# The second layer's input matrix is converted last, through small buffers of its own

## Chip, cores and metric

The kernel runs on one core of one Trainium2 chip. The metric is the device time of one execution in microseconds (us). Engines: PE is TensorE, DVE is VectorE, ACT is ScalarE, POOL is GpSimd, SP is SyncE, which issues the DMAs here.

## What is computed

Attention that keeps the 32 largest scores of each row, then two feed-forward layers with different activations:

```python
scores = q @ k.T / sqrt(64)                       # 4 batches, 8 heads, 576 rows
kth = np.partition(scores, -32, axis=-1)[..., -32:-31]
scores = np.where(scores >= kth, scores, -1e9)
x = softmax(scores) @ v                           # -> 2304 tokens x 512
h = x @ w_in1;  x = np.maximum(0.01 * h, h) @ w_out1        # 512 -> 2048 -> 512
h = x @ w_in2;  r = np.maximum(h, 0)
out = (s * r * r + b) @ w_out2                    # 512 -> 2048 -> 512
```

All is float32. The kernel gets near it from float16 products: each operand is split into a high and a low half (hi, lo), and a product is three matmuls, hi·hi + hi·lo + lo·hi.

## The kernel before

**Attention.** The 2304 tokens are 18 tiles of 128 rows; tiles 4 and 13 each take the last 64 rows of two batches (half-array matmuls). A tile has 4 units of two heads, so there are 72 units, numbered 0 to 71. Of each unit PE makes the scores (`qk`, L1056), ACT copies them out (`s_ev`, L1062), and DVE finds the 32 largest per row: for each head four `MAX8` (L1074) and three `MATCH_REPLACE8` (L1083). ACT and POOL, or for some units DVE (`mask`, L1099), make the masked exponentials; `e_hi` (ACT) and `e_lo` (POOL) split them, a transposing DMA turns them, `pv_mm` (PE, L1224) multiplies with v, and `x_ev` (DVE, L1231) writes the tile's quarter of x.

**The weights.** The four matrices, named 1i, 1o, 2i, 2o (layer, in or out), are converted at the start beside the first tiles of attention, each as 16 units of 128x1024 words (64-bit inputs in, 128x512 float32 kept). A unit is loaded into ring `raw` (`w_load`, L543), brought to float32 (`w_rest` and `w_sign` on ACT, `w_shift` on DVE, `w_round` on POOL), and after four units a Gram matrix on PE (`w_norm`, L594) and some tiny DVE steps give the scale of the group. With it the unit is split into hi and lo. Table `WM` names the way for each unit: A (scale and hi on ACT, lo on POOL), D (hi on ACT, `lo_d` on DVE, L701), G (scale on DVE, hi on ACT, lo on POOL), P and V (a float32 matmul `lo_t` on PE, L706, hi on ACT, lo on PE and ACT for P, on DVE for V). Layer 1's halves stay in SBUF in `wreg`. Layer 2's go to DRAM (`w_out`, L749, tensors `sc16`) out of a ring `hl` of 8, and are streamed back for each block.

`ORDER` (L29) says in which order the matrices pass: 2o, 2i, 1i, 1o. The rings overlay each other: `hl` and the float32 units (`wT`) of 2o, 2i and 1i lie in `wreg` itself, so layer 1's halves can be written only as layer 2's are gone; 1o has a ring `T` of 10.

**The layers.** `layer(i, l, ...)` (L1309) works on one tile for layer 1 (l = 0) and on a block of two tiles for layer 2 (l = 1). PE makes h from x and w_in (`m_in`, L1349), ACT applies the activation from PSUM (`a1`, L1378 and L1381), for layer 2 the square is made twice (`a3`, in float32, on ACT at L1388 or POOL at L1390 as table `SQ` says, and `a4`, its high half), POOL makes the low half (`a5`, L1397), and PE multiplies with w_out (`m_out`, L1419). `finals1` (L791 to L795, DVE) makes layer 1's activation scales, once 1i and 1o have theirs; `finals` (L809 to L823) makes layer 2's, once all matrices are converted and written. `a1` of layer 1 can't start before `finals1`, nor that of layer 2 before `finals`. At `finals` the conversion's buffers close and those of the stream open (`open_phase`). Ring `xT1` holds layer 2's input for two blocks, so layer 1 can be at most four tiles ahead of layer 2.

**The order.** Every step is given to `Plan.add` with its engine and the steps it depends on; `Plan.order` (L311) then emits all of them by a table of ranks, `AT` (L90 to L255), held back only by dependencies and free buffers. So the order of each engine's and of SP's instructions is fixed by numbers, and each engine works its queue strictly in that order.

Of the kernel before, what the change touches and what calls it, by code (L numbers as in the profile page):

```python
# [1530 lines left out]
```

## Time and profile before

| | |
|---|---|
| median of 3 runs | 1139.66 us (1135.37 to 1141.71) |
| the profiled execution | 1141.21 us |
| its span on the core | 1139.1 us |
| mean granted TensorE clock | 0.953 of full speed |
| PE busy | 1041.4 us, 91% of the span |
| DVE busy | 913.2 us, 80% |
| ACT busy | 874.4 us, 77% |
| POOL busy | 797.6 us, 70% |

The span is what the trace shows; the profiled execution's time has 2.1 us around it. An engine's share is an average over stages: conversion with attention, then attention with layers, then layers alone. Waits tell more than shares.

### The profile page before, as it was taken

To read this page: it belongs to the slowest core of one execution; us is meant where nothing else is said; L and a number is where in the kernel's file an instruction comes from. 1 tells how busy PE (TensorE), PEld (TensorE's weight loads), DVE (VectorE), ACT (ScalarE), POOL (GpSimd) and SP (SyncE) were. 2 spreads that over 40 slices of the span, in tenths; PEclk is the share of its full clock that TensorE was granted. 3 is DMA by queue.
4 is the path that set the end of the run, shared out by engine and by line. 5 is a ranking of instruction groups with operands and counts; after the bars stand their busy time and mean duration, and the time that the engine had idled before them with its cause. 6 is when DMAs were issued, how large, how long until landed. Compare 5 with 4: busy or idle time off the path is not lost.

```text
span 1139.1 us, 27433 instructions
## 1 busy us (share of the span) xinstructions
PE 1041.4 (91%) x10254; PEld 727.4 (64%) x10254; DVE 913.2 (80%) x2209; ACT 874.4 (77%) x1653; POOL 797.6 (70%) x1126
## 2 busy tenths in 40 slices
PE   3667676789989999999999999999999999999998
PEld 2334333476756677777767777777777777677665
DVE  3999999999977999999989999982999999710000
ACT  7898999988776977888997986887679677733332
...
PEclk9878688599989999999999999999999999999999
...
GB/s 274 292 179 212 248 310 247 118 81 96 175 152 265 166 102 165 219 150 115 146 224 208 137 238 149 97 101 220 151 158 227 145 81 75 190 160 29 156 188 146
DMA packets 352549, 193.43 MB, mean 170 GB/s; under 512 B 284576, under 2 KB 309152, under 8 KB 352416
## 3 DMA queue, kind: packets, MB, share of 16 engines
...
## 4 chain that ended last, share of the span: by engine, by line
PE 60%; DVE 15%; ACT 11%; DMA 6%; POOL 5%; issue 3%; SPq 1%; DVEq 0%; ACTq 0%; POOLq 0%
PE h L1349 26%; PE acc L1419 24%; DVE mx L1074 5%; DVE wk L1083 4%; PE sc L1056 4%; PE pv L1224 4%; DMA a<-ehl 2%; ACT em L1115 1%; POOL em L1112 1%; DMA st_i<-sc_2i 1%; POOL ehl L1190 1%; DVE wreg L556 1%; DVE em L1099 1%; ACT ehh L1184 1%; DMA late<-in_moe_w_out_dram 1%
## 5 line engine op out<-in xcount | busy, mean ns | idle before, releaser
L1074 DVE MAX8 mx<-wk 128x8 f32<-128x576 f32 x432 | 314.9, 750 | 1.6
L1419 PEld LDWEIGHTS <-late 128*128 128x128 f16 x1728 | 160.4, 98 | 135.0 <-issue 3.0
L1349 PEld LDWEIGHTS <-wreg 128*128 128x128 f16 x3456 | 210.1, 98 | 40.2 <-issue 3.9
L1349 PE MATMUL h<-early,wreg 128*128 128x128 f16 x3456 | 227.5, 220 | 3.0 <-ACT late L1378 2.2
L1419 PE MATMUL acc<-wreg,late 128*128 128x512 f16 x864 | 218.8, 379 | 0.0
L1083 DVE MATCH_REPLACE8 wk<-mx,wk 128x576 f32<-128x576 f32 x288 | 212.9, 743 | 0.0
L1190 POOL TENSOR_TENSOR ehl<-em,ehh 128x576 f16<-128x576 f32 x136 | 175.7, 1296 | 32.0 <-ACT ehh L1184 17.6
L1419 PE MATMUL acc<-st_o,late 128*128 128x512 f16 x756 | 191.6, 380 | 0.5 <-DMA st_o<-sc_2o 0.5
L1349 PE MATMUL h<-late,st_i 128*128 128x256 f16 x1512 | 182.9, 274 | 1.7 <-DMA st_i<-sc_2i 1.7
L1349 PEld LDWEIGHTS <-st_i 128*128 128x128 f16 x1512 | 147.7, 99 | 37.6 <-DMA st_i<-sc_2i 4.7
L1112 POOL TENSOR_TENSOR em<-s,em 128x576 f32<-128x576 f32 x98 | 139.2, 1433 | 26.0 <-ACT em L1109 25.5
L1397 POOL TENSOR_TENSOR late<-early,late 128x512 f16<-128x512 f32 x72 | 84.1, 1168 | 88.4 <-ACT early L1388 54.1
L1397 POOL TENSOR_TENSOR late<-late 128x512 f16<-128x512 f32 x72 | 85.2, 1185 | 47.2 <-ACT late L1394 47.2
L1074 DVE MAX8 mx<-s 128x8 f32<-128x576 f32 x144 | 107.3, 750 | 10.5 <-ACT s L1062 9.8
L1062 ACT COPY s<-sc 128x576 f32<-128x576 f32 x144 | 91.2, 633 | 29.9 <-PE sc L1056 29.7
L1056 PE MATMUL sc<-kT,qT 128*128 128x288 f16 (+1 forms) x640 | 98.4, 294 | 9.5 <-ACT s L1062 6.8
L1083 DVE MATCH_REPLACE8 wk<-mx,s 128x576 f32<-128x576 f32 x144 | 106.8, 743 | 0.0
L1394 ACT ACTIVATE late<-late 128x512 f16<-128x512 f32 x144 | 90.0, 626 | 9.8 <-PE acc L1419 8.1
L1381 ACT ACTIVATE late<-h,cg 128x512 f32<-128x512 f32 x72 | 49.2, 684 | 62.4 <-PE h L1349 61.9
L1184 ACT CAST ehh<-em 128x576 f16<-128x576 f32 x136 | 90.3, 668 | 5.6 <-DVE em L1099 4.9
L1109 ACT ACTIVATE em<-s,st 128x576 f32<-128x576 f32 x98 | 74.1, 771 | 25.6 <-POOL st L1103 25.2
L1115 ACT ACTIVATE em<-em,st,est 128x576 f32<-128x576 f32 x98 | 84.7, 864 | 9.6 <-POOL em L1112 9.0
(217 smaller groups left out, 1657.5 us busy)
## 6 DMA issues: line engine op xcount, KB each, us to landing
...
qn<-in_q_dram SPq DMA_DIRECT2D x16, 256.0 KB, 3.9
sc_2o<-wreg SPq DMA_DIRECT2D x16, 256.0 KB, 4.7
sc_2i<-wreg SPq DMA_DIRECT2D x16, 256.0 KB, 5.5
out_dram<-o SPq DMA_DIRECT2D x16, 256.0 KB, 2.5
```

Source lines behind the costliest of these rows:

```text
L1056: nc.tensor.matmul(pt[a, c, 0:288], lhsT=qT[u][:, h, z, a], rhs=kT[b, p][:, 576 * h + 288 * c:576 * h + 288 * c + 288], start=(z == 0), st ...
L1062: nc.scalar.copy(sc[u, h], box["pt"][:, :, 0:288])
L1074: nc.vector.max(out=mx[u][:, h, r, :], in_=wk[u, h] if r else flat(sc[u, h]))
L1083: nc.vector.match_replace(out=wk[u, h], in_to_replace=mx[u][:, h, r, :], in_values=src, imm_value=NEG)
L1112: nc.gpsimd.tensor_tensor(em[u][:, h, :], flat(sc[u, h]), em[u][:, h, :], op=ALU.subtract)
L1115: nc.scalar.activation(em[u][:, h, :], em[u][:, h, :], AF.Exp, bias=st[u][:, h:h + 1], scale=est[:, 0, u:u + 1], accum_out=st[u][:, 2 + h: ...
L1184: nc.scalar.copy(ehl[u][0][:, 576 * h:576 * h + 576], em[u][:, h, :])
L1190: nc.gpsimd.tensor_tensor(ehl[u][1][:, a], em[u][:, h, :], ehl[u][0][:, a], op=ALU.subtract)
L1349: nc.tensor.matmul(box["h"][:, n * T:(n + 1) * T], lhsT=w[:, ew, c, :], rhs=src[:, ex, c, :], start=(c == 0 and ew == 0 and ex == 0), stop ...
L1394: nc.scalar.activation(gt[:, 0], box["r1"], AF.Square if l else AF.Copy)
L1397: nc.gpsimd.tensor_tensor(ghl[i, l, g][:, 1], box["v"], ghl[i, l, g][:, 0], op=ALU.subtract)
L1419: nc.tensor.matmul(accs[i, l, tt], lhsT=ghl[i, l, g][:, eg, n * T + tt * P:n * T + (tt + 1) * P], rhs=w[:, ew], start=(f == 0 and eg == 0 ...
```

## The change

ORDER becomes 2o, 1i, 1o, 2i. So `finals1` needs only what is converted before 2i, and layer 1 of the first tiles can run while 2i is still converted. For that 2i no longer uses `wreg`: its raw units have a ring `raw2` of 2 (the shared `raw` goes from 5 to 4), its float32 units take ring `T` (from 10 to 8, after 1o), and its halves go out of a ring `hl2` of 1 for ways A, D and G, or in place for V and P. Besides: one group of 2o (units 4 to 7) is brought to float32 by three DVE steps (`w_bits`, `w_top`, `w_tail`) in place of the ACT, DVE and POOL steps; the ways of the units change (`WM`); three of four squares of layer 2 move from ACT to POOL (`SQ`); tables `MK`, `MKE`, `KVM`, `IDM` and `WR` shift a few steps between engines; and `AT` is new throughout. The durations in the `add` calls play no part once `AT` is given.

```diff
-... "xT1": 2, "r1": 2, "r2": 2, "g": 3, "raw": 5, "T": 10, "hl": 8, "wT": 24, "wst": 4,
+... "xT1": 2, "r1": 2, "r2": 2, "g": 3, "raw": 4, "raw2": 2, "T": 8, "hl": 8, "hl2": 1, "wT": 24, "wst": 4,
...
-WM = {"1i": "PPPPPVVPPVPVGVVV", "1o": "ADAAADGAAAAAADAG", "2o": "VPVVPPVVAPVVVPVV", "2i": "PPPPPPPGGPPPPAPA"}
-ORDER = ("2o", "2i", "1i", "1o")
-WJ = {"1i": "SSSS", "1o": "SSSS", "2o": "SSSS", "2i": "SSSS"}
+WM = {"1i": "PPPPGGVPPVPGGDDD", "1o": "AAAAAGPAAAAAAPPP", "2o": "PVVVVPPVAPVGVVPP", "2i": "AAADADADDVVDVVDD"}
+ORDER = ("2o", "1i", "1o", "2i")
+WJ = {"1i": "SSSS", "1o": "SSSS", "2o": "SBSS", "2i": "SSSS"}
...
-SQ = "AAAA"
-MK = "AADADA"
-MKE = "AADAADDADAAAAAAADADAAAAD"
-KVM = "DGDGGDGDDGGGGGGG"
+SQ = "GGAG"
+MK = "DAAADA"
+MKE = "DAAAADDADAAAAAAADADAADAD"
+KVM = "DGDGGGDDDGGGGGGG"
...
 AT = [
-    0, 7, 9, 12, 13, 2, 14, 15, 16, 17, 3, 18, 20, 21, 23, 4, 24, 31, 25, 32, 38, 39, 50, 51, 52, 75, 79, 81, 93, 94, 117, 80, 85, 98, 101, 111,
...
-    PHASED = ("wst", "raw", "T", "nred")
+    PHASED = ("wst", "raw2", "T", "nred")
...
-              "wT": (flat_w, 8 * 512), "hl": (flat_w, 0), "cI": (early, 2560),
+              "wT": (flat_w, 8 * 512), "hl": (flat_w, 0), "hl2": (early, 2048), "cI": (early, 2560),
...
-        w = wreg[:, f + (NU if m[1] == "o" else 0), :] if m[0] == "1" else hl[m, f]
+        w = wreg[:, f + (NU if m[1] == "o" else 0), :] if m[0] == "1" else hl.get((m, f), wT[m, f])
...
-            t = ring("raw", [P, 1024], I32, f"raw_{m}_{f}")
+            t = ring("raw2" if m == "2i" else "raw", [P, 1024], I32, f"raw_{m}_{f}")
...
-            wT[m, f] = ring("T" if m == "1o" else "wT", [P, 512], F32, f"T_{m}_{f}")
+            wT[m, f] = ring("T" if m in ("1o", "2i") else "wT", [P, 512], F32, f"T_{m}_{f}")
...
+        if m == "1i" and f >= 8:
+            modes = [x if x in "PV" else "V" for x in modes]
...
-            out_tok = [token("hl")] if m[0] == "2" else []
+            out_tok = [token("hl")] if m == "2o" else [token("hl2")] if m == "2i" and mode in "GAD" else []
...
-                free = [lo_done["1i", ff]]
-            elif m == "1i":
-                free = [lo_done["2i", ff]] if ff >= 8 else [out_done[order[24 + ff]], cs_done.get(order[24 + ff])]
+                free = [lo_done["2o", 8 + ff] if ff < 8 else lo_done["1i", ff - 8]]
+            elif m == "1i" and ff < 8:
+                free = [out_done["2o", 8 + ff], cs_done.get(("2o", 8 + ff))]
```

What moves, at three places. The first is DVE just ahead of `finals1`, whose first row is the `TENSOR_REDUCE` of `consts`. Before:

```order
L497 TENSOR_SCALAR cg_89<-gram_1o_3_2370 128x1
L718 TENSOR_TENSOR wreg_64<-wlo_1i_15_2399,wreg_64 128x512
L502 TENSOR_SCALAR cg_89<-cg_89 128x1
L1074 MAX mx_11_2404<-s_11_1_2416 128x8
L1083 MATCH_REPLACE wk_11_0_2409<-mx_11_2404,wk_11_0_2409 128x576
L1083 MATCH_REPLACE wk_11_1_2483<-mx_11_2404,s_11_1_2416 128x576
L1074 MAX mx_11_2404<-wk_11_0_2409 128x8
L1074 MAX mx_11_2404<-wk_11_1_2483 128x8
L1083 MATCH_REPLACE wk_11_0_2409<-mx_11_2404,wk_11_0_2409 128x576
L1083 MATCH_REPLACE wk_11_1_2483<-mx_11_2404,wk_11_1_2483 128x576
L786 TENSOR_REDUCE consts_88<-cg_89 128x1
```

and now:

```order
L494 TENSOR_SCALAR cg_89<-gram_1o_3_1830 128x1
L1076 MAX mx_8_1800<-wk_8_0_1807 128x8
L499 TENSOR_SCALAR cg_89<-cg_89 128x1
L719 TENSOR_TENSOR wreg_64<-wlo_1i_13_1856,wreg_64 128x512
L553 SCALAR_TENSOR_TENSOR T_2i_0_1869<-raw_2i_0_197,rest_2i_0_1870 128x512
L719 TENSOR_TENSOR wreg_64<-wlo_1i_12_1816,wreg_64 128x512
L1085 MATCH_REPLACE wk_8_1_1859<-mx_8_1800,wk_8_1_1859 128x576
L1233 TENSOR_TENSOR x32_1_1617<-pv_6_1880,st_6_1458 128x128
L553 SCALAR_TENSOR_TENSOR T_2i_1_1876<-raw_2i_1_218,rest_2i_1_1877 128x512
L1076 MAX mx_8_1800<-wk_8_1_1859 128x8
L1076 MAX mx_9_1974<-s_9_0_1952 128x8
L788 TENSOR_REDUCE consts_88<-cg_89 128x1
```

`finals1` has moved from the middle of unit 11's search to that of units 8 and 9, and only two units of 2i have reached float32 ahead of it. The second place is DVE just ahead of `finals`. Before:

```order
L1074 MAX mx_16_3502<-wk_16_0_3537 128x8
L1083 MATCH_REPLACE wk_16_1_3562<-mx_16_3502,wk_16_1_3562 128x576
L1231 TENSOR_TENSOR x32_3_3296<-pv_14_3642,st_14_3093 128x128
L1074 MAX mx_16_3502<-wk_16_1_3562 128x8
L1139 RECIPROCAL st_15_3322<-st_15_3322 128x2
L1074 MAX mx_17_3726<-s_17_0_3670 128x8
L1099 SCALAR_TENSOR_TENSOR em_16_3703,st_16_3503<-s_16_0_3405,mx_16_3502,em_16_3703 128x576
```

and now:

```order
L1076 MAX mx_19_4408<-wk_19_1_4464 128x8
L719 TENSOR_TENSOR T_2i_12_3706<-wlo_2i_12_4469,T_2i_12_3706 128x512
L1085 MATCH_REPLACE wk_19_1_4464<-mx_19_4408,wk_19_1_4464 128x576
L702 SCALAR_TENSOR_TENSOR early_63<-T_2i_15_4156,cg_89,early_63 128x512
L1085 MATCH_REPLACE wk_19_0_4425<-mx_19_4408,wk_19_0_4425 128x576
L1076 MAX mx_19_4408<-wk_19_1_4464 128x8
L1076 MAX mx_19_4408<-wk_19_0_4425 128x8
L1085 MATCH_REPLACE wk_19_1_4464<-mx_19_4408,wk_19_1_4464 128x576
```

`finals` has moved back from the end of unit 16 to that of unit 19, right behind the last halves of 2i. The third place is ACT in the middle of 2i's halves (`early` is where `hl2` lies). Before, where P units take two ACT copies out of PSUM into a ring of 8:

```order
L712 CAST wreg_64<-wlo_2i_9_1537 128x512
L712 CAST wreg_64<-wlo_2i_10_1554 128x512
L552 ACTIVATE rest_1i_11_1616<-late_65 128x512
L1096 ACTIVATE em_6_1609<-s_6_1_1436,st_6_1401,est_94 128x576
L715 CAST wreg_64<-wlo_2i_9_1537 128x512
```

and now:

```order
L688 ACTIVATE early_63<-T_2i_3_2234,cg_89 128x512
L1186 CAST ehh_13_3193<-em_13_3106 128x576
L1117 ACTIVATE em_13_3106,st_13_2788<-em_13_3106,st_13_2788,est_94 128x576
L1064 COPY s_15_0_3204<-sc_15_0_3145 128x576
L1186 CAST ehh_13_3193<-em_13_3106 128x576
L1064 COPY s_15_1_3221<-sc_15_1_3210 128x576
L686 CAST early_63<-T_2i_4_2598 128x512
```

The high half of unit 4 stands six ACT rows behind that of unit 3 and writes the same buffer.

## Rows read from the trace of the kernel before

**Rows 1.** The page, parts 1 and 2: engines, and PE and its clock in 40 slices
```profile
PE 1041.4 (91%) x10254; PEld 727.4 (64%) x10254; DVE 913.2 (80%) x2209; ACT 874.4 (77%) x1653; POOL 797.6 (70%) x1126
...
PE   3667676789989999999999999999999999999998
...
PEclk9878688599989999999999999999999999999999
```

**Rows 2.** Windows: stretch, length, then PE, PEld, DVE, ACT, POOL busy us; PEclk; DMA share
```profile
0.00:57.00 57.00, 29.95 (x125) 16.66 (x126) 36.95 (x98) 46.52 (x93) 31.53 (x46) 0.91 0.96 283
57.00:232.40 175.40, 124.97 (x812) 70.37 (x811) 171.97 (x415) 165.96 (x322) 138.78 (x185) 0.76 0.80 217
232.40:307.00 74.60, 70.12 (x870) 52.22 (x867) 71.72 (x166) 62.10 (x119) 67.36 (x89) 0.98 0.51 99
307.00:370.00 63.00, 56.91 (x545) 40.05 (x546) 49.37 (x122) 45.52 (x92) 38.98 (x68) 0.95 0.87 220
370.00:769.00 399.00, 393.39 (x4354) 288.69 (x4353) 381.73 (x931) 335.56 (x638) 322.91 (x480) 1.00 0.75 158
769.00:1139.10 370.10, 366.07 (x3558) 259.39 (x3556) 201.51 (x481) 218.77 (x394) 198.06 (x262) 1.00 0.59 148
```

**Rows 3.** Timeline of DVE: last row of finals1, first and last of finals
```profile
236.28 1.14 DVE L795 SCALAR_TENSOR_TENSOR cg<-cg 128x4 f32<-128x4 f32 x1
...
299.78 0.15 DVE L786 TENSOR_REDUCE consts<-cg 128x1 f32<-128x4 f32 x1
...
306.08 0.16 DVE L822 TENSOR_TENSOR consts<-consts,sb 128x1 f32<-128x1 f32 x1
```

**Rows 4.** Timeline of PE: layer 2's first matmuls
```profile
307.00 1.47 PE L1349 MATMUL h<-late,kept_i 128*128 128x256 f16 x12 [0.47 <-issue]
```

**Rows 5.** The chain in order of time: start, us, engine and line, count; pieces at full pace
```profile
81.56 1.72 PE wlo_2o L706 x2
...
308.68 1.32 DVE mx L1074 x2
310.00 1.46 DVE wk L1083 x2
...
412.70 1.34 PE h L1349 x24
414.04 1.94 PE acc L1419 x9
...
763.02 1.87 PE pv L1224 x52
```

**Rows 6.** Groups by line: busy us, mean ns of one, idle before
```profile
L1397 POOL TENSOR_TENSOR late<-early,late 128x512 f16<-128x512 f32 x72 | 84.1, 1168 | 88.4 <-ACT early L1388 54.1 <-ACT late L1394 27.2 <-issue 5.9
L1388 ACT ACTIVATE early<-late 128x512 f32<-128x512 f32 x72 | 44.7, 621 | 1.2
L565 ACT ACTIVATE late<-late 128x512 f32<-128x512 f32 x52 | 35.1, 684 | 0.8
L556 DVE SCALAR_TENSOR_TENSOR wreg<-late,rest_2i 128x512 int32<-128x512 int32 x13 | 8.5, 671 | 0.0
L552 ACT ACTIVATE rest_2i<-late 128x512 int32<-128x512 uint16 x13 | 8.3, 647 | 1.0 <-DVE wreg L556 0.9
L701 DVE SCALAR_TENSOR_TENSOR wreg<-T_1o,cg,wreg 128x512 f16<-128x512 f32 x3 | 3.0, 985 | 0.3 <-ACT wreg L687 0.3
```

**Rows 7.** Timeline of DVE at the start: the first conversion step
```profile
7.62 0.69 DVE L556 SCALAR_TENSOR_TENSOR wreg<-late,rest_2o 128x512 int32<-128x512 int32 x1 [6.45 <-ACT rest_2o L552]
```

**Rows 8.** Waits from 306 to 372 us: total, times, longest
```profile
DVE x L1231 <- PE pv L1224: 5.0, 1, 5.0
DVE cqt L497 <- ACT qj L992: 4.9, 1, 4.9
```

**Rows 9.** The page, part 6: DMA issues, KB, us from issue to landing
```profile
sc_2i<-wreg SPq DMA_DIRECT2D x16, 256.0 KB, 5.5
out_dram<-o SPq DMA_DIRECT2D x16, 256.0 KB, 2.5
```

More of the change, by code (lines that the diff above doesn't have):

```diff
@@ L431, in ring @@
         return pl.tile(shape, dtype, tag=name, name=label, bufs=BUFS[name])
-    SIZE = {"kn": 640, "vn": 640, "xT0": 512, "r2": 512, "hl": 512, "raw": 1024, "wT": 512, "cI": 128, "r1": 512, "g": 512, "xT1": 1024}
+    SIZE = {"kn": 640, "vn": 640, "xT0": 512, "r2": 512, "hl": 512, "hl2": 512, "raw": 1024, "wT": 512, "cI": 128, "r1": 512, "g": 512, "xT1": 1024}
     plan = Plan(BUFS)
@@ L599, in w_diag @@
                                            accum_out=nrm[:, col:col + 1])
-        tr, tT = token("raw"), token("T" if m == "1o" else "wT")
+        tr, tT = token("raw2" if m == "2i" else "raw"), token("T" if m in ("1o", "2i") else "wT")
         if first:
@@ L606 @@
         if whole:
-            x = add(DVE, 0.57, w_bits, [l], kk, take=[tT], use=[tr])
-            x = add(DVE, 0.63, w_top, [x], kk, use=[tT, tr], lock=True)
-            x = rounded[m, f] = add(DVE, 0.63, w_tail, [x], kk, use=[tT, tr], lock=True)
+            tR = token(RB)
+            x = add(DVE, 0.62, w_bits, [l], kk, take=[tT, tR], use=[tr])
+            x = add(DVE, 0.63, w_top, [x], kk, use=[tT, tr, tR])
+            x = rounded[m, f] = add(DVE, 0.62, w_tail, [x], kk, use=[tT, tr, tR])
         else:
@@ L667 @@
             c_ = add(DVE, 0.07, c_half, [c_], kc)
-        i_ = (add(ACT, 0.22, sc_id, [c_], kc, take=tI) if IDM[m][gi] == "A" else add(DVE, 0.25, sc_id, [c_], kc, take=tI, lock=True)) if tI else None
+        i_ = (add(ACT, 0.22, sc_id, [c_], kc, take=tI) if IDM[m][gi] == "A" else add(DVE, 0.3, sc_id, [c_], kc, take=tI, lock=True)) if tI else None
         scaled[m, gi] = c_
@@ L675, with halves @@
             tT = tTs[ff % 4]
-            out_tok = [token("hl")] if m[0] == "2" else []
-            def halves(m=m, ff=ff):
-                if m[0] == "2":
-                    hl[m, ff] = ring("hl", [P, 512], F32, f"hl_{m}_{ff}")
+            out_tok = [token("hl")] if m == "2o" else [token("hl2")] if m == "2i" and mode in "GAD" else []
+            def halves(m=m, ff=ff, mode=mode):
+                if m == "2o" or m == "2i" and mode in "GAD":
+                    hl[m, ff] = ring("hl" if m == "2o" else "hl2", [P, 512], F32, f"hl_{m}_{ff}")
             def hi(m=m, ff=ff, mode=mode, halves=halves):
@@ L722 @@
             if m == "1o":
-                free = [lo_done["1i", ff]]
-            elif m == "1i":
-                free = [lo_done["2i", ff]] if ff >= 8 else [out_done[order[24 + ff]], cs_done.get(order[24 + ff])]
+                free = [lo_done["2o", 8 + ff] if ff < 8 else lo_done["1i", ff - 8]]
+            elif m == "1i" and ff < 8:
+                free = [out_done["2o", 8 + ff], cs_done.get(("2o", 8 + ff))]
             else:
                 free = []
+            free = [x_ for x_ in free if x_ is not None]
             if mode in "GAH":
@@ L733 @@
                 x = add(ACT, 0.613, hi, [c_, *free], ks, use=[tT], take=out_tok)
-                y = add(DVE, 0.663, lo_d, [x], ks, use=[tT] + out_tok, lock=True)
+                y = add(DVE, 0.85, lo_d, [x], ks, use=[tT] + out_tok, lock=True)
             else:
                 th = token("h")
-                x = add(PE, 1.3, lo_t, [i_, *free], ks, take=[th] + out_tok, use=tI + [tT])
-                x = add(ACT, 0.478, hi_p, [x], ks, use=[th] + out_tok)
+                x = add(PE, 1.45, lo_t, [i_, *free], ks, take=[th] + out_tok, use=tI + [tT])
+                x = add(ACT, 0.5, hi_p, [x], ks, use=[th] + out_tok)
                 if mode == "V":
@@ L776, in cfin @@
                         nc.vector.scalar_tensor_tensor(bc, gram["cs", gi], t, bc, op0=ALU.mult, op1=ALU.add)
-                cs_last = add(PE, 0.7, csum, [y, cs_last], ks, take=[] if ff % 4 else [tcs], use=out_tok + ([tcs] if ff % 4 else []))
+                cs_last = add(PE, 0.75, csum, [y, cs_last], ks, take=[] if ff % 4 else [tcs], use=out_tok + ([tcs] if ff % 4 else []))
                 cs_done[m, ff] = cs_last
@@ L795, in finals1 @@
         nc.vector.scalar_tensor_tensor(cg[:, 0, 3, :], cg[:, 0, 2, :], 2.0 ** -12, cg[:, 1, 2, :], op0=ALU.mult, op1=ALU.mult)
-    fin1 = add(DVE, 1.2, finals1, [x for e, x in scaled.items() if e[0][0] == "1"], -100.0)
+    fin1 = add(DVE, 1.2, finals1, [x for e, x in scaled.items() if e[0][0] == "1"] + [rounded["2o", f] for f in range(NU)], -100.0)
     khl, kT, vn, vhl, cv = {}, {}, {}, {}, {}
@@ L1088 @@
                 if r == 0:
-                    ex.append(add(POOL, 0.1, t_neg, [mxd[h], esd], kr, use=[tm]))
+                    ex.append(add(POOL, 0.14, t_neg, [mxd[h], esd], kr, use=[tm]))
                 if r < 3:
-                    mrd[h] = add(DVE, 0.757, t_rep, [mxd[h]], kr, take=[] if r else [tw[h]], use=[tm] + ([tw[h]] if r else [ts[h]]))
+                    mrd[h] = add(DVE, 0.745, t_rep, [mxd[h]], kr, take=[] if r else [tw[h]], use=[tm] + ([tw[h]] if r else [ts[h]]))
         for h in range(2):
@@ L1121 @@
                 x_exp = x
-                mk.append(add(DVE, 0.73, mask, [x, mxd[h]], key + 0.8, use=[te, ts[h], tm], lock=True))
+                mk.append(add(DVE, 0.9, mask, [x, mxd[h]], key + 0.8, use=[te, ts[h], tm], lock=True))
             else:
@@ L1433, in layer @@
                         dep.append(lo_done["1o", f])
-                    out_last = add(PE, 0.665, m_out, dep, kg + 0.002, take=take, use=use)
+                    out_last = add(PE, 0.66, m_out, dep, kg + 0.002, take=take, use=use)
                     if f == NU - 1:
```

37 lines of the change are left out of this document (18 added, 19 removed), and 326 rows, old and new, of the table AT.

## Prediction

> **What bounds the kernel now.** First the engine shares and the slices [rows 1]: PE is busy 91%, and from the tenth slice on nearly every digit is a 9, while the first nine show 3 to 8 and a granted clock of 0.5 to 0.9. So the kernel is bound by PE behind about 250 us, and what PE loses, it loses at the start. The windows put sizes on it [rows 2]: from 307.0 us to the end (832.1 us) PE is busy 816.4 and idle 15.7; from 0 to 307.0 it is busy 225.0, much of that at half clock. DVE is the engine that is full early: 171.97 of 175.4 us between 57 and 232.4, 71.72 of 74.6 up to 307, and ACT is at 95% in the first of these. The reader should see that the end is the time at which layer 2 may start, plus the PE work that is left then, plus PE's idle time behind it. Layer 2 starts when DVE reaches `finals`, from 299.78 to 306.2 us [rows 3]; its first matmul runs at 307.00 [rows 4]. DVE didn't stand waiting for the conversion there: it simply came to those rows.
>
> So there are three terms: how much later `finals` comes, how much more PE has done by then, and what PE idles afterwards. I sum against the profiled execution (span 1139.1 us, time 1141.2, which is 1.5 above the median of 1139.66) and take the difference to the median. 0.5% is 5.7 us, about what a measurement can tell.
>
> **Term 1: `finals` is later.** I counted DVE's rows ahead of `finals` in the program's order, before and now, and priced the differences at full pace [rows 5]: two MAX8 in 1.32 us, two MATCH_REPLACE8 in 1.46. MAX8 goes from 137 to 160 (+23, 15.2 us), MATCH_REPLACE8 from 102 to 120 (+18, 13.1 us). These belong to units 17 to 19, which now come first. `lo_d` goes from 3 to 7 (+4 at 0.985 [rows 6], 3.9 us); two more `mask` at about 1.1 (2.2); two more `lo_v` (1.4); v and k halves, three more `x_ev` and fourteen tiny rows (6.3, less 0.5 for one scaling). Four shifts fall away (4 × 0.671, 2.7 us [rows 6]); the twelve steps of `w_bits` and its two followers come in. The trace does not have them; the nearest row is the shift, the same shape on the same engine, so 12 × 0.67 is 8.1 us. The sum is +47.0.
>
> Of this the 8.1 us of the twelve steps lie in the first 57 us, where DVE is busy 36.95 and idle 20.05 [rows 2], waiting for ACT's part of this same conversion (6.45 us ahead of its first step alone [rows 7]). I take them as hidden: +38.9. If that cover is gone, the term is +47.0. The other end: the four units no longer need ACT's two steps (4 × (0.647 + 0.684) = 5.3 us [rows 6]) at a time when DVE waits for ACT, so it could be +33.6. I take +39, because the waiting is there to be filled and only the second half of the relief depends on what else ACT has queued. `finals` then starts at 338.7 and ends at 345, and layer 2's first matmul runs at 346.
>
> `finals1`, by the same count, has 50 us less DVE work ahead of it, the hidden twelve steps left out (21 MAX8, 18 MATCH_REPLACE8 and 18 shifts are 39 of it, the rest is masks, halves and tiny rows); it ended at 237.4 [rows 3] and would end near 187. This is the change's point, but it pays only through the next term.
>
> **Term 2: PE has done more by then.** PE work ahead of layer 2's first matmul, in order, at full clock: a layer 1 `m_in` matmul takes 0.056 us (24 in 1.34), an `m_out` matmul 0.216 (9 in 1.94), a pv matmul 0.036 (52 in 1.87), `lo_t` 0.86 [rows 5]; scores of 288 columns go by the `m_out` rate, 0.122. `m_in` rises from 576 to 768 (+10.7 us) and `m_out` from 129 to 192 (+13.6): four whole tiles of layer 1 instead of nearly three. Scores rise by 48 (+5.9), pv by 162 half-array matmuls (+5.8), tiny ones by 0.3. `lo_t` falls from 42 to 36 (-5.2) and the P units' second matmul from 25 to 17 at 0.216 (-1.7). So 29.4 us more is done, and as the 6.9 us of conversion are gone for good, 36.3 us less is left. The four tiles are the most there can be: ring `xT1` lets layer 1 be no further ahead. Can PE do it in time? Between 187 and 346 us it has 126 us of work (196 ahead of layer 2's first matmul less 70 ahead of layer 1's, by the same prices) for 159 us; it fits, if the clock is granted.
>
> **Term 3: idle behind it.** Of PE's 15.7 us after 307.0, 6.1 lie between 307 and 370, where DVE idles 13.6 as well [rows 2]: units 16 to 19, the split tile, wait crosswise for PE and ACT [rows 8]. In the new order these units run ahead of `finals`, among conversion steps that can fill such waits, and PE starts layer 2 with four tiles ready. I take 4 us off the 15.7. The ends: 10 off (only the last output and a little remain) and 6 more (waits of the same kind elsewhere).
>
> Other edits I cost at nothing, under PE's cover: the squares on POOL (54 of them; ACT gives up 54 × 0.621 us, POOL gets 54 times about 1.17, by its two-input row of the same size [rows 6]), the few shifted k, v and mask steps, the smaller ring `raw`. If POOL's cover is gone, it is a rival, below.
>
> **The sum.** 39 - 36.3 - 4 = -1.3 us, so 1137.8 us of span and **1138.4 us** against the median: no change that can be told. With the ends, 33.6 - 36.3 - 10 gives 1127 and 47 - 36.3 + 6 gives 1156.
>
> **Rival 1: faster.** The relief of ACT at the start carries through (5.3 us off term 1), and the split tile's waits all vanish (6 instead of 4 off term 3). That gives 1138.4 - 5.3 - 2 = 1131 us. For it speaks that ACT and DVE are both full from 57 to 232 and that DVE's waits at the start are all for ACT. Against it: the same chains cross engines in a fixed order, and a wait taken away in one place tends to appear in another.
>
> **Rival 2: slower, by the single buffer `hl2`.** Twelve units of 2i pass their halves through one buffer. It is free again only when `w_out` has landed. With the measured landing of 5.5 us [rows 9], one cycle is 0.6 (hi) + 1.2 (lo) + 5.5 = 7.3 us. ACT's rows between two such hi's number 9, 8, 8, 6, 15, 20, 13, 8, 25, 17 and 8; at ACT's mean of 0.53 us a row [rows 1] and 90% load, eight rows are 4.7 us. Six of the eleven gaps are too short, by about 2.0, 2.6, 2.6, 3.7, 2.5 and 2.5 us, 16 in all. ACT works in order, so it stands, with the copies of scores and the exponentials behind it, for which DVE and PE wait. ACT has some 10% slack over 159 us, so about 9 of the 16 reach `finals`: 1147.5 us. It decides from a landing of about 3 us on. The output store of the same size lands in 2.5 us [rows 9], and then nothing is short by more than 0.7. Which holds depends on the traffic: the 5.5 us stem from a stretch with a DMA share of 0.80; between 232 and 307 it is 0.51 [rows 2].
> The Trainium skill (DMA: Bandwidth & Descriptors, "Anatomy of one DMA") puts a transfer at about 2.0 us fixed plus its bytes at 436 GB/s, an estimate of 2.6 us for 256 KB; it agrees with the store's row and not with that of `sc_2i`. By it this rival's price is nothing, by the row it is 9 us.
>
> **Rival 3: slower, by POOL.** From 370 to 769 us POOL is busy 322.91 of 399 us; half of the 63 us of squares would make that 355, or 89%. POOL's steps stand in the path of every unit's exponentials and of every group's low half. If a third of the 54 squares cost their extra 0.55 us on PE's path, that is 10 us: 1148. Against it speaks that PE has a second group's h in hand, and that the step POOL waits longest for is the very ACT square that moves (54.1 us [rows 6]).
>
> **Rival 4: layer 1 does not fit.** From 57 to 232 us the granted clock was 0.76 with PE busy 71% [rows 2], a mix of its two levels, 1.2 and 2.4 GHz; from 232 to 307, with layer 1 running, 0.98. If PE's 126 us ahead of `finals` run at 0.76, they need 166 us for the 159 there are, and layer 2 starts some 8 us late: 1146. I hold the second stretch to be nearer, as the added work is layer 1 itself.
> The Trainium skill (TensorE: Matmul & The Clock Gate, "Part 1: The HAM clock gate") says the default is the half clock and that sustained activity lifts it. Bursts of layer 1 with waits between would by that run partly at half clock; no run here shows that stretch yet.
>
> **Chances.** The forecast 0.39, rival 1 0.33, rival 2 0.14, rival 3 0.09, rival 4 0.05. A little of the forecast's own spread falls on either side of the band: faster by over 0.5% 0.35, the same 0.38, slower 0.27. The range leaves out a tenth at each end: 1125 to 1155 us; the forecast's own is 1132 to 1145.
>
> **What would show it.** Right: `finals1` ends near 187, `finals` starts near 339, the first matmul of layer 2 runs near 346 with `m_out` of tile 3 done, and PE idles 12 us or less behind it. Rival 1: `finals` starts before 334. Rival 2: ACT waits for `sc_2i` DMAs or for POOL's low half ahead of the hi's, several us in all, and `finals` starts behind 345. Rival 3: PE's waits ahead of `m_out` for POOL grow from a few us to ten. Rival 4: a clock well below 0.9 from 187 to 346. I am wrong if PE is not nearly full behind layer 2's start, since then the sum of the three terms isn't the end.

## The result, and the profile after: 1.1% slower

| | before | after |
|---|---|---|
| median | 1139.41 us (4 runs, 1135.37 to 1141.71) | 1152.96 us (4 runs, 1149.35 to 1153.28) |
| ratio | | 1.0109, 95% interval 1.0086 to 1.0131 |
| the profiled execution's span | 1139.1 us | 1151.2 us |
| `finals1` ends | 237.4 us | 194.7 us |
| `finals` starts | 299.8 us | 349.8 us |
| layer 2's first matmul | 307.0 us | 354.5 us |
| from there to the end, PE busy and idle | 816.4 and 15.7 us | 780.9 and 15.8 us |

The forecast was no change, 1138.4 us; the kernel is 13.5 us slower, still inside the range, but outside the forecast's own of 1132 to 1145. In the page of the kernel after, its first part and two lines of the slices (the span in 40), PE is full from the fourteenth slice on (from the tenth before [rows 1]), and POOL has more to do:

```profile
PE 1033.3 (90%) x10234; PEld 725.1 (63%) x10234; DVE 915.1 (79%) x2220; ACT 840.8 (73%) x1589; POOL 848.4 (74%) x1175
...
PE   3567757897797999999999999999999999999998
...
PEclk9768768999999999999999999999999999999999
```

The windows of the kernel after answer to [rows 2] (stretch, length, then busy us of PE, PEld, DVE, ACT, POOL; granted clock; DMA share):

```profile
0.00:57.00 57.00, 26.80 (x121) 15.50 (x122) 38.41 (x103) 41.28 (x84) 24.74 (x41) 0.90 0.93 278
57.00:194.70 137.70, 94.13 (x622) 55.15 (x620) 131.78 (x315) 124.01 (x243) 106.34 (x141) 0.74 0.66 181
194.70:349.80 155.10, 129.12 (x1465) 90.76 (x1466) 143.18 (x338) 136.90 (x265) 135.65 (x193) 0.94 0.74 162
354.50:417.00 62.50, 59.10 (x528) 43.03 (x526) 58.78 (x155) 45.53 (x86) 48.90 (x66) 0.97 0.85 227
417.00:769.00 352.00, 345.77 (x3793) 252.68 (x3791) 328.34 (x797) 275.01 (x520) 291.37 (x427) 1.00 0.71 155
769.00:1151.20 382.20, 376.00 (x3668) 265.99 (x3666) 210.25 (x499) 214.04 (x385) 238.40 (x307) 1.00 0.59 149
...
354.50:1151.20 796.70, 780.88 (x7984) 561.70 (x7981) 597.37 (x1450) 534.59 (x991) 578.67 (x798) 1.00 0.66 158
```

And from the timelines of DVE and PE, answering to [rows 3, 4], the last row of `finals1`, the first and last of `finals`, and layer 2's first matmuls:

```profile
194.53 0.15 DVE L797 SCALAR_TENSOR_TENSOR cg<-cg 128x4 f32<-128x4 f32 x1
...
349.84 0.15 DVE L788 TENSOR_REDUCE consts<-cg 128x1 f32<-128x4 f32 x1
...
354.58 0.16 DVE L824 TENSOR_TENSOR consts<-consts,sb 128x1 f32<-128x1 f32 x1
...
354.52 2.78 PE L1351 MATMUL h<-late,kept_i 128*128 128x256 f16 x24
```

So the three terms can be read off. Layer 2 starts 47.5 us later (354.5 against 307.0); PE has 35.5 us less left to do (816.4 against 780.9); its idle time behind the start is 0.1 us longer. 47.5 - 35.5 + 0.1 is 12.1, the difference of the spans. Term 2 was forecast at 36.3 and held. Term 1 was forecast at 39 and term 3 at -4: these two make the error. (`finals` itself starts 50.1 us later; its own rows take 4.9 us where they took 6.5, and layer 2's first matmul runs just ahead of their end instead of 0.8 us behind it.)

The reader should look at the stretch between `finals1` and `finals`. The change's promise shows there: PE is busy 129.12 us at a clock of 0.94, with layer 1 of four tiles. But DVE, which I took to be full on its way to `finals`, is idle 11.9 of 155.1 us. Before, in the same stretch of the program, it was idle 2.4 of 62.4 (windows of the kernel before; the first line is the rest of the way to `finals1` behind [rows 2]'s second stretch):

```profile
232.40:237.40 5.00, 2.67 (x41) 2.33 (x38) 4.86 (x11) 2.79 (x6) 4.92 (x8) 1.00 0.73 144
237.40:299.80 62.40, 60.72 (x752) 45.52 (x752) 60.01 (x139) 56.41 (x108) 57.00 (x75) 0.97 0.46 86
```

What DVE waited for (after, 194.7 to 349.8 us: total, times, longest) is spread over the other engines, ACT first:

```profile
DVE T_2i L553 <- ACT rest_2i L549: 3.2, 7, 1.0
DVE ckt L494 <- PE ksp L856: 2.4, 1, 2.4
DVE mx L1076 <- ACT s L1064: 1.6, 2, 1.4
DVE pw L494 <- ACT xhl L1269: 1.5, 2, 1.2
DVE cg L494 <- PE gram_2i L639: 1.0, 2, 0.9
```

The chain of waits that ends at `finals` (start, us, engine and line) changes its engine every few rows. Summed by engine from 194.7 to 349.8 us, its pieces are 38 us on PE, 33 on POOL, 30 on ACT, 20 in transfers of `raw_2i` and `sc_2i`, and only 14 on DVE; before, in the same stretch of the program, DVE held 26 of 62 us. (Where two steps end almost together, the chain shows only the later one, so it is one of several near-equal chains.) It goes through the small rings: a load of `raw_2i` starts when POOL's rounding frees a buffer, `hi` of the next unit waits for the landing of `sc_2i`, and a tiny matmul that DVE waits for stands behind 72 matmuls of layer 1 in PE's queue:

```profile
275.36 1.15 POOL T_2i L566
276.53 5.10 DMA raw_2i<-in_moe_w_in_dram
...
305.48 4.50 DMA sc_2i<-early
...
316.93 6.50 PE h L1351 x72
323.42 0.17 PE ksp L856 x2
```

### The profile page after: what moved, and what is told of

It reads as the page before. It is cut to its first block, busy times and chain, and to the rows that moved or that the text cites. A ratio compares the mean times of both kernels' runs of the same rounds, so it can differ in the third digit from the quotient of the medians.

```text
span 1151.2 us, 27354 instructions
## 1 busy us (share of the span) xinstructions
PE 1033.3 (90%) x10234; PEld 725.1 (63%) x10234; DVE 915.1 (79%) x2220; ACT 840.8 (73%) x1589; POOL 848.4 (74%) x1175
## 4 chain that ended last, share of the span: by engine, by line
PE 52%; DMA 11%; POOL 10%; ACT 10%; DVE 10%; issue 4%; SPq 2%; DVEq 0%; POOLq 0%; ACTq 0%
PE acc L1421 22%; PE h L1351 22%; DVE mx L1076 3%; PE pv L1226 3%; PE sc L1058 3%; DVE wk L1085 3%; DMA st_i<-sc_2i 2%; POOL ehl L1192 2%; POOL em L1114 2%; DMA a<-ehl 2%; DMA qn<-in_q_dram 1%; DMA late<-in_moe_w_out_dram 1%; POOL late L1399 1%; ACT s L1064 1%; ACT em L1117 1%
## 5 line engine op out<-in xcount | busy, mean ns | idle before, releaser
L1351 PEld LDWEIGHTS <-wreg 128*128 128x128 f16 x3456 | 216.7, 99 | 52.5 <-issue 5.2
L1351 PE MATMUL h<-early,wreg 128*128 128x128 f16 x3456 | 239.0, 221 | 4.1 <-DVE T_2i L719 3.3
L1421 PE MATMUL acc<-wreg,late 128*128 128x512 f16 x864 | 228.4, 381 | 1.3 <-POOL late L1399 1.3
L1192 POOL TENSOR_TENSOR ehl<-em,ehh 128x576 f16<-128x576 f32 x136 | 175.3, 1291 | 20.8 <-ACT ehh L1186 11.1
L1351 PE MATMUL h<-late,st_i 128*128 128x256 f16 x1512 | 185.3, 274 | 2.6 <-DMA st_i<-sc_2i 2.4
L1114 POOL TENSOR_TENSOR em<-s,em 128x576 f32<-128x576 f32 x96 | 136.5, 1436 | 22.4 <-ACT em L1111 22.2
L1076 DVE MAX8 mx<-s 128x8 f32<-128x576 f32 x144 | 107.9, 750 | 15.7 <-ACT s L1064 15.3
L1058 PE MATMUL sc<-kT,qT 128*128 128x288 f16 (+1 forms) x640 | 100.3, 296 | 18.2 <-ACT s L1064 15.8
L1226 PE MATMUL pv<-vhl,a 128*128 128x64 f16 (+3 forms) x2052 | 81.3, 199 | 17.0 <-DMA a<-ehl 9.8
L1226 PEld LDWEIGHTS <-a 128*128 128x128 f16 (+1 forms) x2052 | 75.6, 102 | 31.2 <-DMA a<-ehl 11.8
```

What stands on the lines that cost most here:

```text
L1058: nc.tensor.matmul(pt[a, c, 0:288], lhsT=qT[u][:, h, z, a], rhs=kT[b, p][:, 576 * h + 288 * c:576 * h + 288 * c + 288], start=(z == 0), st ...
L1076: nc.vector.max(out=mx[u][:, h, r, :], in_=wk[u, h] if r else flat(sc[u, h]))
L1114: nc.gpsimd.tensor_tensor(em[u][:, h, :], flat(sc[u, h]), em[u][:, h, :], op=ALU.subtract)
L1192: nc.gpsimd.tensor_tensor(ehl[u][1][:, a], em[u][:, h, :], ehl[u][0][:, a], op=ALU.subtract)
L1226: nc.tensor.matmul(pt[a, o0:o1], lhsT=ahl[u][za][:, blk * P + a.start:blk * P + a.stop], rhs=vt[:, zv, v0:v1], start=(i == 0 and za == 0 a ...
L1351: nc.tensor.matmul(box["h"][:, n * T:(n + 1) * T], lhsT=w[:, ew, c, :], rhs=src[:, ex, c, :], start=(c == 0 and ew == 0 and ex == 0), stop ...
```

## Experiments

The theory to test: the end is layer 2's start plus the PE work left, and `finals` came late by waits across the engines. Rivals: the twelve `w_bits` steps, the single `hl2`, POOL's squares, or one engine that is simply too full ahead of `finals`. The stretch below is from the start of `finals1`'s last row to the start of `finals`' first row, from each kernel's timeline of DVE; it is 155.3 us in the kernel after (194.53 to 349.84). e1 and e8 change nothing ahead of `finals` and have 154.9 and 153.7, so a difference below some 1.6 us says nothing. Each stretch is read from one traced execution, each time is the median of four to ten.

| kernel | `finals1`, last row | `finals`, first row | stretch | median us | ratio to before, interval |
|---|---|---|---|---|---|
| after | 194.53 | 349.84 | 155.3 | 1152.96 | 1.0109 (1.0086 to 1.0131) |
| e1, squares on ACT | 196.15 | 351.09 | 154.9 | 1151.12 | 1.0098 (1.0078 to 1.0119) |
| e3, no `w_bits` | 195.30 | 349.50 | 154.2 | 1152.07 | 1.0094 (1.0074 to 1.0114) |
| e4, DVE cut | 194.59 | 346.81 | 152.2 | 1146.06 | 1.0052 (1.0032 to 1.0073) |
| e5, two `hl2` | 194.55 | 347.57 | 153.0 | 1153.11 | 1.0103 (1.0082 to 1.0124) |
| e6, PE cut | 196.58 | 351.64 | 155.1 | 1151.15 | 1.0094 (1.0069 to 1.0119) |
| e7, DVE and PE cut | 194.81 | 344.04 | 149.2 | 1147.68 | 1.0073 (1.0044 to 1.0101) |
| e8, later search cut | 196.89 | 350.57 | 153.7 | 1151.25 | 1.0097 (1.0070 to 1.0124) |
| e11, DVE, PE, POOL cut | 195.83 | 345.78 | 149.9 | 1147.38 | 1.0067 (1.0043 to 1.0091) |
| e14, ACT cut | 195.12 | 346.42 | 151.3 | 1149.31 | 1.0087 (1.0055 to 1.0119) |
| e15, all four cut | 194.58 | 341.03 | 146.4 | 1142.10 | 1.0016 (1.0001 to 1.0031) |

**e1: the squares back on ACT.**

```diff
-SQ = "GGAG"
+SQ = "AAAA"
```

> The changed kernel with one table undone: all of layer 2's squares on ACT again, as before. My theory (the end is layer 2's start plus PE's work left, and POOL hides the squares): finals ends where it did (354.7 us), PE idles behind it about as long (14.7 us), the time is 1153 +- 4 us. Rival (POOL's squares cost PE waits): PE's idle time behind layer 2's start falls by 5 us or more, the time is 1143 to 1148.

The interval overlaps that of the kernel after; from layer 2's first matmul (355.77) to the end it is 796.1 us, against 796.7. Rival 3 falls: POOL's extra work is hidden.

**e3: without the three DVE steps.**

```diff
-WJ = {..., "2o": "SBSS", ...}
+WJ = {..., "2o": "SSSS", ...}
...
+AT[50:72] = [17, 44, 53, 47, 58, 23, 62, 68, 65, 77, 31, 70, 82, 76, 88, 38, 78, 92, 84, 95, 104, 114, 122, 125, 126]
```

> The changed kernel with units 4 to 7 of 2o brought to float32 as before, by ACT, DVE and POOL: 12 DVE steps (8.2 us) and one scaling go, 4 DVE shifts (2.7 us), 8 ACT and 4 POOL steps come. Theory A (the twelve steps were not hidden, so that term 1 came out at its upper end): finals1 and finals come about 5.5 us earlier, the time is 1147 to 1149. Theory B (they were hidden in waits, and the missing time is from waits behind finals1): both come where they were or later by up to 5 us, the time is 1152 to 1158.

Theory B. `finals1` is where it was, and in the first 57 us DVE is busy 5.0 us less and idle 5.0 us more (23.6 against 18.6, its window below). So the twelve steps did fill waiting, as the prediction had it, and taking them out gains nothing. But without them DVE waits 23.6 us there where the kernel before waited 20.1 [rows 2]: in the new order it waits longer for other steps.

```profile
0.00:57.00 57.00, 25.50 (x122) 14.92 (x123) 33.38 (x94) 45.53 (x92) 28.84 (x45) 0.94 0.93 276
```

**e4: less search ahead of `finals`.**

```diff
 def t_max(...):
...
+    if u in (17, 18, 19) and r in (1, 2):
+        return
     nc.vector.max(...)
 def t_rep(...):
...
+    if u in (17, 18, 19) and r in (1, 2):
+        return
     nc.vector.match_replace(...)
```

> The changed kernel with the second and third round of the search for the largest left out in units 17 to 19 (so that these keep 16 scores a row, not 32): 12 MAX8 and 12 MATCH_REPLACE8 less on DVE ahead of finals, 24 x 0.74 = 17.7 us, and nothing else. My theory (DVE's queue holds finals, and the end follows finals): finals ends 14 to 18 us earlier (337 to 341), the time is 1135 to 1139. Rival 1 (the conversion of 2i itself, by ACT, POOL and its small rings, holds finals nearly as late): finals only 3 to 8 us earlier, DVE's waits for ACT grow by 10 us, the time is 1145 to 1150. Rival 2 (PE's work ahead of layer 2 is what binds): finals earlier but layer 2's first matmul is not, the time is 1150 to 1153.

Rival 1. Of 17.7 us taken off DVE, 3.1 arrive at `finals` (152.2 against 155.3); DVE idles most of the rest (24.4 us of the stretch instead of 11.9). Its waits between 194.7 and 346.8 us have grown where it waits for ACT and PE:

```profile
DVE early L702 <- ACT early L688: 6.7, 4, 4.5
DVE ckt L494 <- PE ksp L856: 4.4, 1, 4.4
DVE T_2i L553 <- ACT rest_2i L549: 3.8, 7, 1.0
DVE mx L1078 <- ACT s L1064: 2.7, 3, 1.8
```

The second of these waits shows why. From 323.26 to 342.95 us every row of PE starts within 0.01 us of its time in the kernel after, and ACT's rows near there within 0.7 us. So DVE's row behind the tiny `ksp` matmul starts at the same moment with and without the cut (first after, then e4; in brackets its idle time):

```profile
323.63 0.16 DVE L494 TENSOR_SCALAR ckt<-ksp 128x1 int32<-128x1 int32 x1 [2.40 <-PE ksp L856]
...
323.63 0.16 DVE L494 TENSOR_SCALAR ckt<-ksp 128x1 int32<-128x1 int32 x1 [4.43 <-PE ksp L856]
```

The median falls by 6.9 us, more than `finals` moves; layer 2's first matmul is only 1.6 us earlier in the traced execution (352.90), which was the slowest of the six. So up to 6.9 of the 17.7 us reach the end, and what makes up the difference is open.

This is the run that overturns my reading: DVE was the fullest engine of the stretch (92%), and yet its work alone did not set `finals`. The Trainium skill (Perfetto Trace Analysis, "Identifying the Most-Contended Engine") would have the engine with the highest occupancy optimized first. Here that engine gave back at `finals` a sixth of what was taken from it; where three engines are at 87 to 92% the rule doesn't tell which matters, and the measurement decides.

**e5: two buffers for the halves.**

```diff
-"xT0": 4, ... "hl2": 1, ... "hl2": (early, 2048)
+"xT0": 3, ... "hl2": 2, ... "hl2": (early, 1536)
```

> The changed kernel with two buffers hl2 in place of one; the second takes the place of the fourth xT0, so xT0 has 3. ACT stood 2.5 us in all for that buffer ahead of finals, the last time (1.3 us at 310) ahead of a step for which the others then waited. My theory: finals comes 0 to 3 us earlier, the time is 1149 to 1154. Rival (the single buffer costs the 9 us that I forecast): finals ends before 347, the time is 1143 to 1147.

The second buffer takes the place of an `xT0` because with one of its own (e2) the buffers don't fit: one pool wants 24.0 KB a partition, and 20.8 are left. `finals` is 2.3 us earlier, little more than the scatter, and the time is the same; PE idles 18.0 us behind layer 2's start instead of 15.8, which may be the price of the `xT0` (not tried apart). Rival 2 falls, and by its own condition, that it decides from a landing of about 3 us on: in the kernel after the twelve transfers out of `hl2` landed in 2.5 us at the median, not in 5.5 as those of [rows 9] (DMA issues, 194.7 to 349.8 us; KB, us to landing), and ACT stood for the buffer 2.5 us in all (total, times, longest):

```profile
raw_2i<-in_moe_w_in_dram SPq DMA_DIRECT2D x13, 512.0 KB, 4.6
sc_2i<-early SPq DMA_DIRECT2D x12, 256.0 KB, 2.5
...
ACT early L688 <- DMA sc_2i<-early: 1.3, 1, 1.3
ACT early L686 <- DMA sc_2i<-early: 1.2, 1, 1.2
```

The prediction's estimate of 2.6 us by the Trainium skill (DMA: Bandwidth & Descriptors, "Anatomy of one DMA") agrees with this row, though that section gives its figures for DMAs that GpSimd issues, and these are issued by SP.

**e6 to e8: PE's share, both cuts, and a control.**

```diff
 def m_in(...):
...
-    for ew, ex in ((0, 0), (0, 1), (1, 0)):
+    for ew, ex in ((0, 0),) if l == 0 and i in (0, 1, 2, 3) else ((0, 0), (0, 1), (1, 0)):
...
 def m_out(...):
...
-    for eg, ew in ((0, 0), (0, 1), (1, 0)):
+    for eg, ew in ((0, 0),) if l == 0 and i in (0, 1, 2, 3) else ((0, 0), (0, 1), (1, 0)):
...
```

The lines left out close each sum one matmul earlier (`stop`). e7 adds e4's edit; e8 is e4's edit with units (30, 31, 32).

> The changed kernel with layer 1 of the first four tiles made of hi.hi alone, one matmul of three: 512 m_in and 128 m_out matmuls less on PE, 28.6 + 27.6 = 56 us ahead of layer 2, the order untouched. Theory A (DVE's queue alone holds finals): finals where it was (354.7), and so is the time, 1151 to 1155. Theory B (in the new order no engine alone holds it: the conversion and the search wait crosswise, among other things for small matmuls that stand behind layer 1 in PE's queue): finals comes 2 to 6 us earlier and the time falls by as much, to 1147 to 1151.

> Both cuts at once: layer 1 of the first four tiles made of hi.hi alone (56 us of PE less) and the search of units 17 to 19 without its second and third round (17.7 us of DVE less). Theory A (after DVE's cut it is PE's queue that holds finals): finals comes a good deal earlier than with the one cut, below 342. Theory B (a chain across all engines in fixed order): the two gains about add up, 2.5 us and 2 to 6 us, finals ends between 344 and 350, the time is 1141 to 1146.

> A control for the cut of units 17 to 19: the same two rounds left out in units 30 to 32, whose search comes when PE is full with layer 2. If the time follows layer 2's start: no effect, 1151 to 1155 us, finals at 354.7. If DVE's load counts anywhere: 3 us or more faster, below 1150.

The cut of 56 us at full clock takes less than that off PE's time. In e6's stretch (window below) the granted clock is 0.74, a mix of the two levels 1.2 and 2.4 GHz, where it was 0.94 in the kernel after; PE is busy 97.8 us instead of 129.1, so 31 us less:

```profile
196.70:351.60 154.90, 97.84 (x873) 65.82 (x874) 143.36 (x339) 136.28 (x265) 136.65 (x193) 0.74 0.70 163
```

PE idles 57 us there instead of 26, and the stretch does not change by anything that can be told (155.1 us). So PE's queue by itself does not hold it, and rival 4, a clock or a load that PE can't meet, falls with it. My expectation for e6 (2 to 6 us) was wrong. With DVE cut as well (e7) the stretch is 149.2: 6.1 off, 2.8 more than the sum of the two, and `finals` ends at 349.3, as theory B had it, though the time is 1147.7 and not below 1146. So far as one trace each can tell, neither engine held it alone: with DVE's work gone its rows stand behind PE's (e4), with PE's gone nothing moves. The control moves nothing that can be told: its interval overlaps that of the kernel after, where e4's does not.

**e11, e14, e15: POOL and ACT.** e11 is e7 and this; e14 has the second edit alone; e15 has everything.

```diff
 def a5(...):
+    if l == 0 and i in (0, 1, 2, 3):
+        return
...
 def above(...):
+    if 8 <= u < 20:
+        return
...
 def less(...):
-    nc.gpsimd.tensor_tensor(em[u][:, h, :], flat(sc[u, h]), em[u][:, h, :], op=ALU.subtract)
+    nc.gpsimd.tensor_tensor(em[u][:, h, :], flat(sc[u, h]), flat(sc[u, h]) if 8 <= u < 20 else em[u][:, h, :], op=ALU.subtract)
```

> Three cuts at once: the search of units 17 to 19 without its second and third round (DVE), layer 1 of the first four tiles from hi.hi alone (PE), and its low halves not made at all (16 steps of 1.17 us, 18.7 us less on POOL). With the first two the stretch from finals1 to finals fell from 155.3 to 149.2 us. Theory A (POOL, 92% busy there, is what then holds it): it falls below 144 us. Theory B (no engine alone; the single steps stand in a fixed order and wait for each other and for the small rings): it falls by 0 to 4 us more, to 145 to 149.

> The changed kernel without ACT's step that marks the scores below the 32nd largest, in units 8 to 19 (their weights are then not masked): 18 steps of 0.77 us, some 12 us less on ACT at full pace, nothing else. Theory A (ACT is what holds the stretch from finals1 to finals, 155.3 us): it falls by 5 us or more, below 150, and the time by as much, to 1143 to 1148. Theory B (no engine alone): it falls by 0 to 3 us, the time is 1149 to 1154.

> All four cuts at once: ACT's marking step of units 8 to 19, two rounds of the search of units 17 to 19 on DVE, two of three layer 1 matmuls of the first four tiles on PE, and those tiles' low halves on POOL. Without ACT's cut the stretch was 149.8 us, with ACT busy 91% of it and the others at 84% or less. Theory A (ACT held it then): it falls below 143 us. Theory B (what is left are chains in the fixed order and small rings, raw2 and hl2): 145 to 150 us.

Theory A falls in e11 and e15. In e11 the stretch is 149.9 us, no shorter than e7's 149.2, so 18.7 us less on POOL bring nothing on top; e15's 146.4 lies where theory B put it. e14 lies between the two (4.0 us off, more than B allowed and less than A asked). Its edit is not ACT's alone, against what I expected: POOL's subtraction no longer waits for ACT's marking, and takes 1.15 us a step instead of 1.44. So the 4.0 us cannot be put down to ACT's load by itself. All four cuts together would take 17.7, 56, 18.7 and 12 us off DVE, PE, POOL and ACT at full pace, and the stretch falls by 8.9 us. These windows (e11, then e15) leave out the last microseconds of each stretch:

```profile
194.80:344.00 149.20, 97.75 (x864) 65.32 (x865) 125.60 (x301) 135.61 (x263) 117.78 (x176) 0.74 0.71 163
```

```profile
195.00:338.00 143.00, 94.37 (x862) 63.32 (x863) 122.13 (x295) 124.56 (x244) 112.13 (x175) 0.77 0.74 165
```

In e11 ACT is still busy 91%. In e15 nothing is full: ACT is busy 87%, DVE 85%, POOL 78% and PE 66%, and `finals` still starts at 341.0, later than my forecast of 338.7 for the whole work. So no engine's load explains what is left. I put it down to the order, in which each queue waits for steps that another queue has in its place, and to the small rings; that is by exclusion and not shown apart. The chain of e15 from 194.7 to 341 us speaks for the first: its pieces are 38 us on ACT, 29 on POOL, 18 on DVE, 12 on PE, 20 in the turning of the exponentials (`a`), and 10 in transfers of `raw_2i` and `sc_2i`, the two small rings. Larger rings were not run, except for e5: a third `raw2` finds no room in SBUF unless ring `T` gives up two buffers.

**e9, e10: other orders.** Only the table `AT` differs, all 5860 steps, engines and buffers being the same; the ranks come from a search that rearranged the steps so as to shorten the chains ahead of layer 2, as estimated from step lengths like those of the trace.

> The changed kernel with another table AT and nothing else: the ranks were moved by a search over orders that shortens the chains across engines ahead of layer 2 (the same steps, engines, buffers and ways). My theory (what held layer 2's start is not work but the waits across engines, which the order sets): finals1 and finals come 6 to 12 us earlier than in the changed kernel (finals ends before 349), PE's work behind layer 2's start is the same, and the time is 1140 to 1147. Rival (the conversion's and attention's steps fill the engines, so that no order gives more than a microsecond or two): finals ends after 351, the time is 1150 or more.

> As e9_order_a, with the table that the same search found from another start. My theory: 1140 to 1147 us again, finals before 349, by other single moves. Rival: 1150 or more.

Both miss widely: 1177.99 us (1.0336, interval 1.0317 to 1.0355) and 1176.73 us (1.0330, 1.0303 to 1.0358). In e9 `finals1` ends 7.6 us later than in the kernel after (its last row at 202.10), `finals` starts at 359.91 (365.19 in e10), and behind layer 2's start at 366.6 PE idles 24.4 us of 812.4 instead of 15.8 and has 7.1 us more to do. That an order can cost 25 us is shown; that mine would be better is refuted, and whether any order of these steps gains something stays open. No version beat the kernel before.

**e12, e13: what a microsecond of `finals` is worth.**

```diff
-                    nc.vector.max(out=mx[u][:, h, r, :], ...)
+                    for _ in range(17 if (u, h, r) == (19, 1, 3) else 1):
+                        nc.vector.max(out=mx[u][:, h, r, :], ...)
```

e13 has the same in the kernel before, at (16, 1, 3).

> The changed kernel with the last MAX8 of unit 19's search, the last step of that search ahead of finals, made 17 times instead of once: 16 x 0.66 = 10.6 us more on DVE just ahead of finals. It measures what a microsecond of finals is worth. My theory (layer 1 can be no further ahead, so PE stands): layer 2 starts 10.6 us later, its span behind that is unchanged, the time is 1162 to 1165. Rival (what is lost at the start is made good in the 16 us that PE idles later): 1155 to 1159.

> The kernel before with the same delay, at its place: the last MAX8 of unit 16's search made 17 times, 10.6 us more on DVE ahead of its finals. My theory (each engine's order is fixed, so PE takes no later work in its place there either): 9 to 11 us slower than before, 1149 to 1151. Rival (layer 1 isn't at its cap there, so PE has other work to do): 2 to 6 us slower.

After: 1162.97 us, 10.0 more than the kernel after. Before: 1152.45 us, 12.0 more than the 1140.41 measured beside it, a little above what I expected. In the traced executions layer 2's first matmuls are these (e12, then e13):

```profile
366.84 3.97 PE L1352 MATMUL h<-late,kept_i 128*128 128x256 f16 x24
...
317.16 2.51 PE L1350 MATMUL h<-late,kept_i 128*128 128x256 f16 x12
```

In e12 layer 2 starts 12.3 us later and the span is 9.9 longer (1161.1); in e13 both are 10.2 (span 1149.3). So a delay of `finals` is paid four fifths or in full, in either order, and the rival of e12 and e13, that PE makes most of it good later, falls. This is the first step of the argument, and it is shown. For a few microseconds it is no fine scale: over the runs with the order of the kernel after, PE's idle time behind layer 2's start lies between 9.8 us (e7) and 18.0 (e5).

## Why the prediction was wrong

**The frame held.** The end is the time at which layer 2 may start, plus PE's work left, plus its idle time: the three terms add up to the span's difference, and in e12 and e13 a delay of `finals` reaches the end by 9.9 of 12.3 and 10.2 of 10.2 us.

**Term 1 failed, in its count of one engine.** The step was: "I counted DVE's rows ahead of `finals` in the program's order, before and now, and priced the differences at full pace". That prices DVE's work and takes its waiting as given, apart from the 8.1 us to be hidden. It was +47.5 and not +39, and both halves of the pricing were off (windows above and [rows 2]). Ahead of `finals` DVE is busy 313.4 us where it was 273.8: 39.6 more, not 47.0. And it is idle 36.4 us where it was 26.0: 10.4 more, not 8.1 less. So the work was priced 7.4 us too high, the waiting 18.5 too low, and `finals` starts 50.1 us later where 38.9 was forecast. That the 47.5 us come near the count without the hiding (+47.0) is a coincidence.

Part of the work that was counted too high can be named from the rows: twelve masks took 12.2 us where ten had taken 13.4, and seven of the twelve scalings of the identity (L650) are no longer on DVE, 2.2 us that the sum does not list. Of the waiting, the first 57 us were to lose 8.1 us and lost 1.5: e3 shows that the twelve steps are hidden, but DVE waits longer for other steps there. From 57 us to `finals1` it is 2.4 us more. The largest part is between `finals1` and `finals`: 11.9 us of DVE idle where there were 2.4, 9.5 more. I had read "DVE didn't stand waiting for the conversion there: it simply came to those rows", which was true of 62 us in which DVE was 96% busy, and carried it over to 155 us in which 2i's conversion, ACT, POOL and layer 1 share one fixed order. e4 shows it: take away DVE work that I priced, and `finals` moves by a sixth of it. Rows of DVE ahead of a point say how much work comes before it, not when it comes.

**Term 2 held**: 35.5 us against 36.3, `m_out` of tile 3 done just ahead of layer 2's start, as forecast; its counts hold too (768 `m_in`, 192 `m_out`, 36 `lo_t` matmuls ahead of that start). `finals1` ended at 194.7, not near 187, 42.7 us earlier instead of 50: DVE's work ahead of it fell by 43.6 us with the twelve steps in it, and its waiting, which was to take them in, rose by 0.9.

**Term 3 failed in its size**: +0.1, not -4. What I saw does happen: the stretch behind layer 2's start loses waits (6.1 us of PE idle in the first 63 us before [rows 2], 3.4 in the first 62.5 after). But the later stretches give it back: 6.2 us idle from 417 to 769 (5.6 from 370 to 769 before) and 6.2 from 769 on (4.0 before). That is what I had written against rival 1, that a wait taken away in one place appears in another, and I should have applied it to my own term. The term is known to about 2 us: e1, e3 and e8, which keep the work and the buffers ahead of layer 2 or nearly so, have 15.2, 14.8 and 16.2 us.

**The rivals.** Rival 1 (faster) falls with `finals` at 349.8 and not before 334. Rival 2 (single `hl2`) and rival 3 (POOL's squares) were no cause: e5, e1. Rival 4 neither: the granted clock was 0.94 between `finals1` and `finals`, and e6, with 56 us less for PE, starts layer 2 no earlier. The right side was slower, by a rival I did not name: that the new order makes `finals` wait across engines. Its price could not be read from [rows 2], where DVE is 98% busy from 57 to 232 us and 96% from there to 307; 92% on 155 us, as it came out, is 6 us more than 96%.

## What to carry to other kernels

When a step is moved to where several engines are near 90%, don't price its finish by counting one engine's rows: allow for the waits too, and follow the moved step's own chain through all queues and small rings. If work is to be banked ahead of a barrier, ask first what the barrier costs when it comes later; here 10 to 12 us of delay lengthened the span by 10, the barrier came 47.5 us later, and the bank took only 35.5. And test the count before trusting it: a cut of the work on the engine that seems to hold the path is one run, and tells whether it does. Look in the cut's trace at what it did to the other engines as well: here it changed PE's clock (e6) and a step of POOL (e14).

## What else the runs showed

Tiny DVE rows took seven to eight times their length beside POOL. Two rows of `finals` of 128x4 elements took 1.26 and 1.33 us in the kernel after (timeline of DVE), just while POOL's two subtractions ran from 351.03 to 353.83; in e4, with no POOL row at that time, the same two took 0.17 and 0.16.

```profile
351.23 1.26 DVE L817 TENSOR_SCALAR cg<-cg 128x4 int32<-128x4 int32 x1
352.52 1.33 DVE L818 SCALAR_TENSOR_TENSOR cg<-cg 128x4 f32<-128x4 f32 x1
```

```profile
351.03 2.80 POOL L1114 TENSOR_TENSOR em<-s,em 128x576 f32<-128x576 f32 x2 [0.89 <-ACT em L1111]
```

The Trainium skill (SBUF — State Buffer, "Who interferes with whom") says that DVE and GpSimd share a pair of ports, that a DVE instruction with two SBUF inputs or in a mode that uses both ports contends for it, and that the one that comes second is blocked for the whole of the other's instruction. The rows agree in that each of the two DVE rows ends within 0.1 us of a POOL subtraction; which mode the first, with one input, ran in no row shows.
